# Sliding-window attention with top-1 experts on one core: q, k and v laid out by the host, bias added with the maximum

## The chip, the cores and the metric

The kernel runs on one core of one Trainium2 chip. The metric is device time in microseconds (us): the median of three timed runs of the kernel before is 689.68 us (685.45 to 692.1). The engines are TensorE (PE, with its weight loads PEld), VectorE (DVE), ScalarE (ACT), GpSimd (POOL) and SyncE (SP), which only issues transfers here.

## The reference

Eight batches, eight heads, 576 positions, 64 values a head. Scores get a bias that falls with distance, and only the 128 positions up to the query's own are seen. The rows of the result (4608 tokens x 512) go through a top-1 mixture of eight experts.

```python
scores = scale * np.matmul(q, k.transpose(0, 1, 3, 2))
rel = pos[:, None] - pos[None, :]
bias = slopes[:, None, None] * (-np.abs(rel).astype(np.float32))[None, :, :]
mask = (rel >= 0) & (rel < window)              # window = 128
scores = np.where(mask, scores + bias[None], -1000000000.0)
scores = scores - np.max(scores, axis=-1, keepdims=True)
attn = np.exp(scores)
attn = attn / (np.sum(attn, axis=-1, keepdims=True) + 1e-09)
x = np.matmul(attn, v)                          # then (tokens, heads * 64)
# per token: expert = argmax of cosine with expert_emb, gate = softmax at it
out[mask] = gate_w[mask, None] * (np.maximum(x[mask] @ w1[e], 0.0) @ w2[e])
```

## The kernel before, in words

The program has two stages. The first is attention with routing, 36 tiles of 128 query rows: per batch four tiles of 128 rows (the first of a batch is of kind "first", the others "full"), and per pair of batches one tile of kind "pair", which holds the last 64 rows of both. A tile is done in two halves of four heads, so there are 72 half tiles, called u below. The second stage runs the experts one after the other on the rows that routing scattered into a table in device memory. Part of the first expert's work (384 rows, "head") is done within the first stage, once 24 tiles are routed.

A half tile goes through these steps, each of which is a job of a planner:

- load (SP): q, k and v of the tile, 128 rows x 8 heads x 64, in runs of 64 values (`load`, L413 and L416).
- turn and copy (PE, then ACT or DVE): q and k are transposed four heads' pairs at a time by `prep_pe` (L492) into a PSUM bank and copied to SBUF by `prep_copy` (ACT L528, DVE L526), q with the scale.
- score (PE, `score_pe`): for two banks j a product writes the bias first (L592: the tables of `factors` for full and pair tiles, `tab_first` through the identity for first tiles), then L598 adds q times k, in fp32, over up to 256 key columns.
- merge (DVE, `merge_dve`, L607 and L610): the 256 columns hold the previous and the own tile's keys; a predicated copy folds them into 128, one per bank j.
- max (DVE, `max_dve`, L615): one reduction per bank, for two heads.
- exp (ACT, L622, one per head), flip (PE, L630, four transposes), phi (ACT, L481: the probabilities' high halves in fp16), plo (DVE, L484: the low halves), mask (POOL, L650 and L663: splits the folded block again), av (PE, `values_pe`, L698: 24 products), and the normalisation (DVE, L714 and L720).
- per tile: high and low halves of the result (ACT L734 or DVE L736, POOL L747), its square norm (ACT L743), a transposing transfer (SP, L751), the logits (PE, L757 and L761; DVE, L770), then for a group of tiles the routing (DVE and ACT, L825 to L854) and one scattering transfer per tile (POOL, L863).

The order on each engine is written by the planner (`Plan.run`): a list scheduler with a table of costs per job. At each step it looks at the engine whose next job can start first, and takes, among the jobs that can start within that engine's `SLACK` of the earliest, the one with the smallest due time. Due times are `STEP * u + 1000 * DUE[stage]`. Rings of buffers bound how far a job may run ahead; the PSUM rings of the first stage are `sc` (4 banks, two per half tile), `ps` (2 banks, shared by flip and av) and `pt` (2 banks, for turns, logits and small products). What the planner writes is a fixed order per engine; at run time each engine takes its instructions strictly in that order.

The costs and the order that touch the change most:

```python
J(f"score{u}", "PE", 750 if first else 1150 if pair else 1250, ...)
for j in range(2):
    J(f"merge{n}", "DVE", 0 if first else 202 if pair else 335, ...)
    J(f"max{n}", "DVE", 335, ..., after=[f"merge{n}"] + ([f"max{u}_0"] if j else []))
J(f"plo{u}", "DVE", 627, lambda a=a: probs_dve(*a), after=[f"phi{u}"], ...)
```

The second stage is not touched.

Of the kernel before, what the change touches and what calls it, by code (L numbers as in the profile page):

```python
# [13 lines left out]
F16 = mybir.dt.float16  # L14
BF16 = mybir.dt.bfloat16
F32 = mybir.dt.float32
# [13 lines left out]
SP_ = 2.0**15  # L30
# [22 lines left out]
STEP = 3038  # L53
SLACK = {'PE': 100, 'ACT': 100, 'DVE': 50, 'POOL': 400, 'SP': 300}
# [5 lines left out]
DUE = {'load': -8.2, 'loadv': 0.0, 'k': -6.5, 'q': -5.1, 'v': 2.1, 'score': -1.3, 'merge': 2.4, 'max': 1.7, 'exp': 3.0, 'flip': 3.2, 'phi': -1.8, 'plo': 7.8, 'mask': 6.2, 'av': -1.9, 'norm': 9.6, 'xhi': 2.6, 'xlo': 12.3, 'xnorm': 10.3, 'xdma': 16.1, 'logit': -1.8, 'route': 15.9, 'put': 19.8, 'place': 15.6, 'gap': 4.3}  # L60
# [8 lines left out]
SHARE = {'v': 0, 'x': 0.25, 'q': 0, 'k': 0, 'v2': 0, 'x2': 0.5, 'q2': 0.5, 'k2': 0.25}  # L69
# [88 lines left out]
def kernel(  # L158
# [12 lines left out]
    B, H, S, D = q.shape  # L171
    NTOK, DM = out.shape
    E, _, F = moe_w1.shape
# [7 lines left out]
    QS = -float(D) ** -0.5  # L181
# [34 lines left out]
    idb = const.tile([P, P], BF16, name="idb")  # L216
    nc.vector.tensor_copy(idb, ident)
# [54 lines left out]
    def merge_mask(kind):  # L272
        mk[kind] = const.tile([P, P], I32, name=f"mask_{kind}")
        nc.vector.tensor_scalar(mk[kind], rels[kind], 0.0, None, op0=ALU.is_ge)

    def first_table():
        tab = const.tile([P, H, P], BF16, name="tab_first")
        for h in range(H):
            nc.vector.tensor_scalar(tab[:, h, :], rels["full"], slopes[h], None, op0=ALU.mult)
        nc.gpsimd.affine_select(  # L280
            tab, tab, pattern=[[0, H], [-1, P]], compare_op=ALU.is_ge, fill=-NEG, base=0, channel_multiplier=1
        )
        tabs["first"] = tab

    def factors():
        at = const.tile([P, 2 * P], F32, name="at")
        nc.gpsimd.iota(at, pattern=[[1, 2 * P]], base=-P, channel_multiplier=0, allow_small_or_imprecise_dtypes=True)
        for kind in ("full", "pair"):
            tabs["row", kind] = const.tile([P, P], BF16, name=f"row_{kind}")
        tabs["col"] = const.tile([P, H // 2, 2 * P], BF16, name="col")  # L290
        for j in range(2):
            two, one = slice(64 * j, 64 * j + 2), slice(64 * j, 64 * j + 1)
            for kind in ("full", "pair"):
                row = tabs["row", kind]
                nc.vector.memset(row[two], 1.0)
                if kind == "full":
                    nc.vector.tensor_copy(row[one], at[one, P : 2 * P])
                else:
                    for i in range(2):
                        nc.vector.tensor_copy(row[one, i * REM : (i + 1) * REM], at[one, P : P + REM])  # L300
            for c in range(H // 2):
                x = slopes[2 * c + j]
                nc.vector.tensor_scalar(tabs["col"][two, c, :], at[two], -x, None, op0=ALU.mult)
                nc.gpsimd.memset(tabs["col"][one, c, :], x)
# [86 lines left out]
    def attention(actx):  # L391
# [11 lines left out]
        loaded = {}  # L403

        def load(T, which="qkv"):
            kind, b, t = tiles[T]
            r = loaded.setdefault(T, {})
            for nm, src in (("k", k), ("q", q), ("v", v)):
                if nm not in which:
                    continue  # L410
                x = ld.tile([P, H, D], F32, tag=f"ld{nm}", name=f"ld{nm}_{T}")
                if kind != "pair":
                    nc.sync.dma_start(x, src[b, :, t * P : (t + 1) * P, :].rearrange("h p d -> p h d"))  # L413
                else:
                    for i in range(2):
                        nc.sync.dma_start(  # L416
                            x[i * REM : (i + 1) * REM], src[b + i, :, NF * P : S, :].rearrange("h p d -> p h d")
                        )
                r[nm] = x

        load(0, "kq")
        load(1, "kq")
# [10 lines left out]
        bias_rel("full")  # L433
        first_table()
        merge_mask("full")
# [42 lines left out]
        qT, kT, vS = {}, {}, {}  # L478
# [6 lines left out]

        prep = {}

        def prep_pe(T, nm):
            x = loaded[T][nm].rearrange("p h d -> p (h d)")
            pt = bank("pt", [P, HP, P], name=f"pt{nm}_{T}")  # L490
            for hp in range(HP):
                nc.tensor.matmul(  # L492
                    pt[:, hp, :],
                    x[:, hp * P : (hp + 1) * P],
                    ident,
                    start=(hp == 0),
                    stop=(hp == HP - 1),
                    is_transpose=True,
                    skip_group_check=True,
                )  # L500
            prep[T, nm] = pt

        def k_blocks(T):
            kind, b, t = tiles[T]
            return [(b, 1), (b + 1, 1)] if kind == "pair" else [(b, t // 2)]

        def fill(T, nm):

            kind, b, t = tiles[T]
            if nm == "q":  # L510
                return [(qT.setdefault(T, {}), slice(0, P), slice(0, P), "q", P)]
            if kind == "pair":
                return [
                    (kT[x], slice(2 * P, 2 * P + REM), slice(i * REM, (i + 1) * REM), "k1", None) for i, x in enumerate(k_blocks(T))
                ]
            x = k_blocks(T)[0]
            return [(kT.setdefault(x, {}), slice(t % 2 * P, t % 2 * P + P), slice(0, P), f"k{x[1]}", 2 * P + REM * x[1])]

        def prep_copy(T, nm):
            scale = QS if nm == "q" else 1.0  # L520
            for at, dst, src, tg, w in fill(T, nm):
                if "x" not in at:
                    at["x"] = qk.tile([P, HP, w], F32, tag=tg, name=f"{nm}_{T}", bufs=KBUFS[tg])
                o_, i_ = at["x"][:, :, dst], prep[T, nm][:, :, src]
                if on_dve(T, nm):
                    nc.vector.tensor_scalar(o_, i_, scale, None, op0=ALU.mult)  # L526
                else:
                    nc.scalar.activation(o_, i_, AF.Copy, scale=scale)  # L528
            del prep[T, nm]

        def on_dve(T, nm):
            return share(T, SHARE[nm if T < LATE else nm + "2"])
# [10 lines left out]
        def v_hi(T):  # L543
            dst = vS[T][0][:, :, 0:D]
            if not share(T, SHARE["v" if T < LATE else "v2"]):
                nc.scalar.activation(dst, loaded[T]["v"], AF.Copy)
            else:
                nc.vector.tensor_copy(dst, loaded[T]["v"])

        def v_lo(T):  # L550
            tg = v_tag(T)
            lo = vp.tile([P, H, D], F16, tag=tg + "o", name=f"vo_{T}", bufs=VBUFS[tg])
            vS[T][1] = lo
            nc.gpsimd.tensor_tensor(lo, loaded[T]["v"], vS[T][0][:, :, 0:D], op=ALU.subtract)
# [13 lines left out]
        def score_pe(T, hf):  # L568
            kind, b, t = tiles[T]
            qx = qT[T]["x"]  # L570
            own = kT[k_blocks(T)[0]]
            if kind == "first":
                spans = [(slice(0, P), slice(0, P), own, slice(0, P))]
            elif kind == "pair":
                spans = [
                    (slice(i * REM, (i + 1) * REM), slice(0, P + REM), kT[x], slice(P, 2 * P + REM)) for i, x in enumerate(k_blocks(T))
                ]
            elif t % 2:
                spans = [(slice(0, P), slice(0, 2 * P), own, slice(0, 2 * P))]
            else:  # L580
                spans = [
                    (slice(0, P), slice(0, P), kT[b, t // 2 - 1], slice(P, 2 * P)),
                    (slice(0, P), slice(P, 2 * P), own, slice(0, P)),
                ]
            for j in range(2):
                ps = sc[T, hf, j] = bank("sc", [P, 2, 2 * P], name=f"sc{j}_{T}_{hf}")
                if kind == "first":
                    a_, b_ = idb, tabs["first"].rearrange("p (c j) k -> p j c k", j=2)[:, j, 2 * hf : 2 * hf + 2, :]
                else:
                    r = slice(64 * j, 64 * j + 2)  # L590
                    a_, b_ = tabs["row", kind][r], tabs["col"][r, 2 * hf : 2 * hf + 2, 0 : spans[-1][1].stop]
# [1080 lines left out]
```

## Time and profile before

| what | us |
|---|---|
| median of the three timed runs | 689.68 |
| the profiled execution's own time | 690.15 |
| its span, from the first to the last instruction | 688.4 |
| around the span | 1.75 |
| mean granted clock of TensorE, share of 2.4 GHz | 0.971 |
| busy over the span: PE, DVE, ACT, POOL | 643.3, 377.8, 340.8, 261.4 |

A row of busy time by stretch gives, for each engine, the time in which at least one of its instructions was under way, and their number in brackets; then the granted clock, the share of the transfer engines that was busy, and GB/s. A vector instruction's recorded duration reaches past the start of the next one where nothing makes that one wait, so a sum of durations is more than the time they take in a row; the starts of neighbours show the latter. PE products are recorded to their modelled end, some tenths of a us behind the next one's start.

### The profile page before, as it was taken

What the parts mean: (1) busy time and instruction counts of PE and PEld (TensorE: products, weight loads), DVE (VectorE), ACT (ScalarE), POOL (GpSimd) and SP (SyncE); (2) the same over time, 40 slices, a digit from 0 to 9 for tenths busy, and PEclk for the clock granted to TensorE, in tenths of its full rate; (3) what the DMA queues carried; (4) which work ended last, traced back from release to release, by engine and by line L of the source; (5) the groups of instructions that cost most, each with busy time, mean ns of one, the idle gap of its engine ahead of it and who ended that gap; (6) DMA issues with size and microseconds to landing.
All of it is one profiled execution on the core that took longest, in us unless ns stands there. A gap on an engine that the chain in (4) does not pass through costs nothing. (4 is left out here: it accounts for less than half of the span.)

```text
span 688.4 us, 15704 instructions
## 1 busy us (share of the span) xinstructions
PE 643.3 (93%) x6043; PEld 425.1 (62%) x6043; DVE 377.8 (55%) x974; ACT 340.8 (49%) x794; POOL 261.4 (38%) x472
## 2 busy tenths in 40 slices
PE   7999999999999988992999999999999999999993
PEld 4777767777776755641665467476584764754442
DVE  5877786776789969642335724344244255310250
ACT  5999888977887955410235523343243244210210
POOL 7667687767777837552010210120111112001011
PEclk9999999998999999886999999999999999999998
DMA  8588969886988895136999973934919545001000
GB/s 200 125 184 191 194 170 206 159 214 129 201 156 229 196 206 161 41 109 149 249 250 358 250 262 55 269 123 67 318 63 240 202 99 200 16 16 47 13 31 31
DMA packets 217676, 109.83 MB, mean 160 GB/s; under 512 B 195829, under 2 KB 195829, under 8 KB 217600
## 3 DMA queue, kind: packets, MB, share of 16 engines
q1 hardware_dynamic: 211760, 89.89, 55.7%
q0 software_dynamic: 5840, 18.92, 7.2%
q8 instruction: 48, 0.79, 0.5%
q14 instruction: 28, 0.23, 0.1%
HBM read 61.92 MB, written 28.12 MB: 131 GB/s over the span
## 5 line engine op out<-in xcount | busy, mean ns | idle before, releaser
L1374 PE MATMUL ps<-xT,w1h 128*128 128x272 f16 (+7 forms) x896 | 175.4, 296 | 13.4 <-DMA xT<-xs 12.2
L1374 PE MATMUL ps<-xT,w1l 128*128 128x272 f16 (+7 forms) x448 | 132.4, 296 | 0.0
L1374 PEld LDWEIGHTS <-w1h 128*128 128x128 f16 x896 | 88.2, 99 | 44.8 <-issue 14.1
L384 POOL DMA_INDIRECT out_dram<-y,ids x32 | 35.6, 1112 | 203.5 <-DVE y L1432 105.3
L1382 DVE SCALAR_TENSOR_TENSOR hl<-ps,hh 128x272 f16<-128x272 f32 (+7 forms) x112 | 51.7, 475 | 105.9 <-ACT hh L1384 99.5
L1384 ACT ACTIVATE hh<-ps 128x272 f16<-128x272 f32 (+7 forms) x112 | 45.6, 425 | 114.7 <-PE ps L1374 114.7
L622 ACT ACTIVATE pe<-sc,nm 128x128 f32<-128x128 f32 x288 | 87.7, 390 | 24.6 <-DVE nm L615 13.7
L1418 PE MATMUL ps<-w2h,hh 128*128 128x512 f16 (+1 forms) x264 | 98.4, 373 | 0.0
L1418 PE MATMUL ps<-w2l,hh 128*128 128x512 f16 (+1 forms) x264 | 98.4, 373 | 0.0
L1418 PE MATMUL ps<-w2h,hl 128*128 128x512 f16 (+1 forms) x264 | 98.4, 373 | 0.0
L1418 PEld LDWEIGHTS <-hh 128*128 128x128 f16 x528 | 51.5, 98 | 58.6 <-issue 0.8
L598 PE MATMUL sc<-k,q 64*128 64x128 f32 (+2 forms) x768 | 74.8, 339 | 0.5 <-ACT q L528 0.5
L484 DVE SCALAR_TENSOR_TENSOR pq<-ptp,pq 128x512 f16<-128x512 f32 x72 | 53.1, 738 | 20.3 <-ACT pq L481 18.1
L598 PEld LDWEIGHTS sc<-k,q 64*128 64x128 f32 (+1 forms) x768 | 51.0, 180 | 19.3 <-issue 16.4
L481 ACT ACTIVATE pq<-ptp 128x512 f16<-128x512 f32 x72 | 55.0, 764 | 14.4 <-PE ptp L630 8.8
L615 DVE TENSOR_REDUCE nm<-sc 128x2 f32<-128x256 f32 x144 | 58.5, 416 | 3.2 <-PE sc L598 2.9
L630 PE MATMUL ptp<-ident,pe 128*128 128x128 f32 x288 | 48.0, 287 | 8.0 <-ACT pe L622 3.6
L1349 DVE SCALAR_TENSOR_TENSOR w2l<-ws,w2h 128x1024 f16<-128x1024 f32 x28 | 33.9, 1223 | 36.2 <-ACT w2h L1351 36.0
L1374 PEld LDWEIGHTS <-w1l 128*128 128x128 f16 x448 | 44.1, 99 | 15.1 <-DVE w1l L1349 0.3
L1349 DVE SCALAR_TENSOR_TENSOR w1l<-ws,w1h 128x1024 f16<-128x1024 f32 x28 | 33.4, 1222 | 34.0 <-ACT w1h L1351 33.9
L747 POOL TENSOR_TENSOR gx<-xf,gx 128x512 f16<-128x512 f32 x36 | 42.7, 1187 | 19.7 <-ACT gx L734 8.5
L698 PE MATMUL av<-vh,mp 128*128 128x65 f16 (+1 forms) x512 | 49.0, 200 | 0.5 <-POOL mp L650 0.5
(233 smaller groups left out, 1174.1 us busy)
## 6 DMA issues: line engine op xcount, KB each, us to landing
ws<-moe_w_dram SPq DMA_DIRECT2D x56, 512.0 KB
ldk<-k_dram SPq DMA_DIRECT2D x32, 256.0 KB
ldq<-q_dram SPq DMA_DIRECT2D x32, 256.0 KB
ldv<-v_dram SPq DMA_DIRECT2D x32, 256.0 KB
stg<-moe_w_dram SPq DMA_DIRECT2D x16, 256.0 KB
xs<-zrow SPq DMA_DIRECT2D x3, 1092.2 KB
xs<-zrow SPq DMA_DIRECT2D x1, 1413.5 KB
xs<-zrow SPq DMA_DIRECT2D x1, 1285.0 KB
```

The costliest lines, as they stand in the source:

```text
L481: nc.scalar.activation(hi, ps, AF.Copy, scale=scale)
L484: nc.vector.scalar_tensor_tensor(lo, ps, scale, hi, op0=ALU.mult, op1=ALU.subtract)
L598: nc.tensor.matmul(sc[T, hf, j][o, l, w], qx[rows, hp, o], at["x"][rows, hp, kc], start=False, stop=(l == 1), skip_group_check=True)
L615: nc.vector.tensor_reduce(nm_t[T, hf][:, j, :], sc[T, hf, j][:, :, 0:P], axis=AX.X, op=ALU.min)
L622: nc.scalar.activation(pr_t[T, hf][:, 2 * l + j, :], ps[:, l, 0:P], AF.Exp, bias=nm[:, l : l + 1], scale=-1.0)
L630: nc.tensor.transpose(pt[:, i, :], pe[:, i, :], ident)
L698: nc.tensor.matmul(o_, a_, b_, start=False, stop=(n == last), skip_group_check=True)
L1349: nc.vector.scalar_tensor_tensor(lo_, x, SW, hi, op0=ALU.mult, op1=ALU.subtract)
L1374: nc.tensor.matmul(ps[:, :w], a[:, kt, fs], xx[:, b + kt, c0 : c0 + w], start=(n == 0), stop=(n == len(jobs) - 1))
L1382: nc.vector.scalar_tensor_tensor(hl[:, ft, c0 : c0 + w], ps[:, :w], 0.0, hi, op0=ALU.max, op1=ALU.subtract)
L1384: nc.scalar.activation(hi, ps[:, :w], AF.Relu)
L1418: nc.tensor.matmul(ps, x[:, ft, a * P : (a + 1) * P], w[:, ft, c], start=(n == 0), stop=(n == len(jobs) - 1))
```

## The change

- The host lays out q, k and v with numpy: q and k transposed, each tile's data in one run per partition. The turns and copies of q and k go (PE, ACT, DVE); q and k are loaded straight to where the products read them, q into 4 buffers of a tile, k into 3 of a batch.
- The bias products go. Two tables in bf16 (`bias_table`) hold the bias of each head after folding, and `max_dve` adds it with the maximum: one `tensor_tensor_reduce` per head writes (score + bias) * (-scale) back to PSUM and the minimum to `nm`. In the built program each is two instructions: the operation and a read of its accumulator (both appear as ISA).
- Both banks of a half tile are one tile of `sc` now (two tiles in place of four), and the four heads are folded by one predicated copy.
- The low halves of the probabilities are made, for each second half tile from u = 52 on (ten in all), by a product that subtracts the high halves in PSUM (`rest_pe`) and a copy on ACT, in place of the DVE operation.
- In pair tiles `av` uses full 128-column weights: POOL writes two masked tiles with a zeroed half each.
- PSUM rings: `sc` 2 x 2 banks, `ps` 3, `pt` 1. `STEP`, `SLACK`, `DUE` and `SHARE` have new values (a line or two shown); all high halves of the result before tile 26 are on ACT.

```diff
-SP_ = 2.0**15
+SP_ = 2.0**14
-RING = {'sc':'sc','pt':'pt','ptp':'ps','av':'ps','lg':'pt','misc':'pt'}
-BANKS = {'sc':4,'ps':2,'pt':2}
+RING = {'sc':'sc','ptp':'ps','av':'ps','lg':'pt','misc':'pt'}
+BANKS = {'sc':2,'ps':3,'pt':1}
-KBUFS = {"k0": 2, "k1": 2, "q": 3}
+KBUFS = {"k": 3, "q": 4}
-STEP = 3038
-SLACK = {'PE': 100, 'ACT': 100, 'DVE': 50, 'POOL': 400, 'SP': 300}
+STEP = 2454
+SLACK = {'PE': 43, 'ACT': 184, 'DVE': 46, 'POOL': 541, 'SP': 31}
-SHARE = {'v': 0, 'x': 0.25, 'q': 0, 'k': 0, 'v2': 0, 'x2': 0.5, 'q2': 0.5, 'k2': 0.25}
+SHARE = {'v': 0, 'x': 0, 'v2': 0, 'x2': 0.5, 'p': 0, 'p2': 0.5}
...
+    def bias_table(kind):
+        rel = rels[kind]
+        m = const.tile([P, P], I32, name=f"mask_{kind}")
+        wrap = const.tile([P, P], F32, tag="wrap", name=f"wrap_{kind}")
+        nc.vector.tensor_scalar(m, rel, 0.0, None, op0=ALU.is_ge)
+        nc.vector.tensor_scalar(wrap, rel, 0.0, float(WIN), op0=ALU.is_lt, op1=ALU.mult)
+        nc.vector.tensor_tensor(wrap, wrap, rel, op=ALU.add)
+        tab = const.tile([P, H, P], BF16, name=f"tab_{kind}")
+        for h in range(H):
+            nc.vector.tensor_scalar(tab[:, h, :], wrap, -slopes[h] / QS, None, op0=ALU.mult)
+        mk[kind], tabs[kind] = m, tab
...
-            for j in range(2):
-                ps = sc[T, hf, j] = bank("sc", [P, 2, 2 * P], name=f"sc{j}_{T}_{hf}")
...
-                nc.tensor.matmul(ps[:, :, 0 : b_.shape[-1]], a_, b_, start=True, stop=False, skip_group_check=True)
+            sc[T, hf] = bank("sc", [P, 2, 2, 2 * P], name=f"sc_{T}_{hf}")
...
-        def merge_dve(T, hf, j):
+        def merge_dve(T, hf):
             kind, b, t = tiles[T]
+            ps = sc[T, hf].rearrange("p j l c -> p (j l) c")
+            w = {"full": P, "pair": REM}.get(kind)
+            if w:
+                m = mk[kind][:, 0:w].unsqueeze(1).to_broadcast([P, 4, w])
+                nc.vector.copy_predicated(ps[:, :, 0:w], m, ps[:, :, P : P + w])
-            nc.vector.tensor_reduce(nm_t[T, hf][:, j, :], sc[T, hf, j][:, :, 0:P], axis=AX.X, op=ALU.min)
+            o_ = sc[T, hf][:, j, l, 0:P]
+            nc.vector.tensor_tensor_reduce(
+                o_, o_, tabs[tiles[T][0]][:, 4 * hf + 2 * l + j, :], -QS, BIG, ALU.add, ALU.min, nm_t[T, hf][:, j, l : l + 1]
+            )
...
+        def rest_pe(T, hf):
+            pq, pt = pq_t[T, hf]
+            nc.tensor.matmul(pt, minus, pq[:, :, :, 1], start=False, stop=True, skip_group_check=True)
+        def probs_lo(T, hf):
+            pq, pt = pq_t[T, hf]
+            if rest_on_pe(2 * T + hf):
+                hi_part(pq[:, :, :, 0], pt, SP_)
+            else:
+                lo_part(pq[:, :, :, 0], pq[:, :, :, 1], pt, SP_)
...
+                J(
+                    f"merge{u}", "DVE", 0 if first else 335 if pair else 600, lambda a=a: merge_dve(*a),
+                    after=[f"score{u}"], uses=[key], due=due("merge", u),
+                )
+                    for l in range(2):
+                        J(
+                            f"max{n}_{l}", "DVE", 245, lambda c=c, l=l: max_dve(*c, l),
+                            after=[f"max{n}_0" if l else f"merge{u}"] + ([] if l or not j else [(f"max{u}_0_0", ORDER)]),
...
+    qt = paired(np.asarray(q).transpose(0, 2, 1, 3)).reshape(-1, P, H // 2, 2 * D).transpose(0, 3, 2, 1)
+    kt = np.asarray(k).reshape(B, H // 2, 2, S // REM, REM, D).transpose(0, 2, 5, 3, 1, 4)
+    vt = paired(np.asarray(v).transpose(0, 2, 1, 3))
```

Three places in the built order. First DVE, first half of tile 10 before and of tile 16 after (both full): `sc0`, `sc1` and `sc` are scores, `nm` the minima, `tab_full` the bias table. Before:

```order
L484 SCALAR_TENSOR_TENSOR pq_9_0_1766<-ptp_9_0_1748,pq_9_0_1766 128x512 [waits Activation_49]
L607 COPY_PREDICATED sc0_10_0_1758<-mask_full_152,sc0_10_0_1758 128x2x128 [waits PE_49]
L770 COPY gl_0_719<-ptl_7_1779 128x16 [waits PE_49]
L615 TENSOR_REDUCE nm_10_0_1799<-sc0_10_0_1758 128x2 [waits DVE_49]
L825 TENSOR_SCALAR rc_0_1817<-gn_0_488 128x8
L607 COPY_PREDICATED sc1_10_0_1760<-mask_full_152,sc1_10_0_1760 128x2x128
L714 RECIPROCAL rs_9_0_1830<-av_9_0_1801 128x4 [waits PE_49]
L615 TENSOR_REDUCE nm_10_0_1799<-sc1_10_0_1760 128x2 [waits DVE_49]
```

After, on the same engine:

```order
L470 SCALAR_TENSOR_TENSOR pq_15_0_2345<-ptp_15_0_2326,pq_15_0_2345 128x512 [waits Activation_49]
L714 COPY gl_1_1817<-ptl_12_2357 128x16 [waits PE_49]
L537 COPY_PREDICATED sc_16_0_2339<-mask_full_139,sc_16_0_2339 128x4x128
L658 RECIPROCAL rs_14_1_2408<-av_14_1_2369 128x4 [waits PE_49]
L543 ISA sc_16_0_2339,nm_16_0_2410<-sc_16_0_2339,tab_full_144 128x128 [waits DVE_49]
L543 ISA nm_16_0_2410 128x1
```

Two folds and two reductions have become one fold and four pairs of operation and accumulator read; three more pairs like the last one follow straight behind, and the operation of each of those waits, in the built program, for the accumulator read just ahead of it.

Second, PE in the middle of the stage (`ptk` and `ptp` are the banks of a turn of k and of a flip, `sc0`, `sc1` scores). Before:

```order
L492 MATMUL ptk_18_2850<-ident_68,ldk_18_2339 128x128 x4
L630 MATMUL ptp_16_0_2861<-ident_68,pe_16_0_2844 128x128 x4
L592 LDWEIGHTS row_pair_172
L592 MATMUL sc0_17_0_2874<-col_173,row_pair_172 128x2x192
L592 LDWEIGHTS row_pair_172
L592 MATMUL sc1_17_0_2876<-col_173,row_pair_172 128x2x192
L598 MATMUL sc0_17_0_2874<-k_11_1815,q_17_2763 64x192
```

After, on PE, from a flip on:

```order
L560 MATMUL ptp_0_3131<-ident,pe_0_3101 128x128 x4
L522 MATMUL sc_0_3141<-k_1755,q_2604 128x256 x4
L560 MATMUL ptp_1_3169<-ident,pe_1_3159 128x128 x4
L627 LDWEIGHTS erow
L627 MATMUL av_1_3176<-eone,erow 128x4
```

Turns and bias products are gone; a flip is followed by scores, and these by the next flip or av.

Third, PE at the end of the attention stage, from the last av product on (`ps_head` is the head expert's output bank, `w1`, `w2` its weights). Before:

```order
L698 LDWEIGHTS mp_1_6354
L698 MATMUL av_1_6409<-vh_4877,mp_1_6354 64x65
L969 LDWEIGHTS hh_head
L969 MATMUL ps_head_6459<-w2h_4951,hh_head 128x512
L969 LDWEIGHTS hh_head
L969 MATMUL ps_head_6459<-w2l_4952,hh_head 128x512
```

After:

```order
L642 LDWEIGHTS mp_35_1_5630
L642 MATMUL av_1_5664<-vh_4947,mp_35_1_5630 128x65
L891 LDWEIGHTS w1h_4388
L891 MATMUL ps_head_5645<-x_head,w1h_4388 128x384
L891 LDWEIGHTS w1l_4389
L891 MATMUL ps_head_5645<-x_head,w1l_4389 128x384
```

Before, all 96 products of the head's first layer stood ahead of the last av; after, 44 of them stand behind it, ahead of the 72 of the second layer.

## Rows read from the trace of the kernel before

**Rows 1.** Busy time by stretch of the span: us, busy time and instructions of PE, PEld, DVE, ACT and POOL, granted clock, transfer share, GB/s.

```profile
20.00:120.00 100.00, 96.73 (x1380) 75.39 (x1380) 78.97 (x237) 88.51 (x237) 71.64 (x116) 1.00 0.82 178
120.00:240.00 120.00, 113.83 (x1613) 87.32 (x1609) 97.87 (x299) 99.47 (x267) 91.14 (x156) 0.97 0.84 184
20.00:240.00 220.00, 210.56 (x2991) 162.71 (x2989) 176.84 (x535) 187.98 (x503) 162.78 (x270) 0.98 0.83 181
240.00:292.00 52.00, 45.09 (x517) 30.54 (x517) 38.84 (x112) 28.07 (x73) 27.17 (x44) 0.91 0.60 136
292.00:326.00 34.00, 21.76 (x114) 10.22 (x113) 11.95 (x62) 2.39 (x8) 12.87 (x31) 0.75 0.48 128
340.00:650.00 310.00, 308.81 (x2066) 187.84 (x2065) 120.83 (x176) 103.85 (x170) 41.00 (x62) 1.00 0.55 161
```

**Rows 2.** The longest wait of PE from 20 to 240 us: who waited for whom, us in total, times, longest.

```profile
PE ptp L630 <- ACT pe L622: 2.1, 3, 0.8
```

**Rows 3.** PE in order of time near 132 us: start, us recorded, line, out<-in.

```profile
131.75 0.63 PE L630 MATMUL ptp<-ident,pe 128*128 128x128 f32 x4
132.22 0.60 PE L492 MATMUL ptq<-ident,ldq 128*128 128x128 f32 x4
132.65 0.38 PE L592 MATMUL sc<-tab_first,idb 128*128 128x256 bf16 x2
132.97 0.71 PE L598 MATMUL sc<-k,q 64*128 64x128 f32 x8
```

**Rows 4.** Busy time of single PE lines from 20 to 240 us: first the bias products (L592), then the turns (L492, four to a turn).

```profile
20.00:240.00 220.00, 24.12 (x124) 0.98 0.83 181
20.00:240.00 220.00, 37.94 (x252) 0.98 0.83 181
```

**Rows 5.** Busy time of single DVE lines from 20 to 240 us, in this order: folds of full tiles (L607), folds of pair tiles (L610), maxima (L615), copies of q and k (L526), high halves (L736), low halves of the probabilities (L484).

```profile
20.00:240.00 220.00, 32.62 (x83) 0.98 0.83 181
20.00:240.00 220.00, 2.96 (x12) 0.98 0.83 181
20.00:240.00 220.00, 49.65 (x124) 0.98 0.83 181
20.00:240.00 220.00, 4.13 (x6) 0.98 0.83 181
20.00:240.00 220.00, 5.76 (x8) 0.98 0.83 181
20.00:240.00 220.00, 45.85 (x62) 0.98 0.83 181
```

**Rows 6.** Groups of DVE instructions over the span: shapes, count, busy us, mean ns of one, idle before.

```profile
L607 DVE COPY_PREDICATED sc<-mask_full,sc 128x256 f32<-128x256 int32 x96 | 37.8, 421 | 2.7 <-PE sc L598 1.9 <-PE ptp L630 0.8
L610 DVE COPY_PREDICATED sc<-mask_pair,sc 128x128 f32<-128x128 int32 x16 | 3.9, 293 | 1.6 <-PE sc L598 1.6
```

**Rows 7.** DVE in order of time: two neighbours near 128 us; the smallest write without a source, near 1 us; two small instructions of the routing, each of which waits for the one ahead, near 304 us.

```profile
128.14 0.50 DVE L610 COPY_PREDICATED sc<-mask_pair,sc 128x128 f32<-128x128 int32 x2
128.54 0.76 DVE L615 TENSOR_REDUCE nm<-sc 128x2 f32<-128x256 f32 x2
...
0.85 0.06 DVE L226 MEMSET eone<- 3x4 bf16 x1 [0.85 <-PEq L1661]
...
303.53 0.16 DVE L829 TENSOR_TENSOR rz<-rz,gn 128x2 f32<-128x2 f32 x1
303.73 0.16 DVE L830 TENSOR_TENSOR rz<-rz,ry 128x2 f32<-128x2 f32 x1
```

**Rows 8.** Busy time by stretch, columns as in rows 1.

```profile
220.00:240.00 20.00, 18.94 (x267) 14.59 (x267) 19.46 (x50) 19.11 (x50) 18.12 (x27) 1.00 0.89 208
240.00:260.00 20.00, 16.90 (x183) 12.00 (x183) 14.40 (x45) 12.82 (x34) 6.12 (x8) 0.91 1.02 198
260.00:280.00 20.00, 17.15 (x196) 10.92 (x195) 16.74 (x47) 10.54 (x30) 15.06 (x29) 0.91 0.44 133
```

**Rows 9.** ACT and POOL: the busy time of ACT's copies of q and k (L528) from 20 to 240 us; two neighbours on ACT near 123 us; the group of POOL's masks of pair tiles.

```profile
20.00:240.00 220.00, 34.12 (x59) 0.98 0.83 181
...
122.79 0.63 ACT L528 ACTIVATE k<-ptk 128x512 f32<-128x512 f32 x1
123.27 0.78 ACT L481 ACTIVATE pq<-ptp 128x512 f16<-128x512 f32 x1
...
L663 POOL TENSOR_SCALAR_AFFINE_SELECT tails<-pq 64x256 f32<-64x256 f32 x16 | 7.0, 436 | 5.6 <-DVE pq L484 4.2 <-DVE rs L714 0.6 <-DVE rz L828 0.3
```

**Rows 10.** The start: DVE makes the first table, POOL masks it (a group of one), PE turns the first k, DVE takes the first maximum.

```profile
2.66 1.18 DVE L279 TENSOR_SCALAR tab_first<-rel_full 128x128 bf16<-128x128 f32 x8 [0.87 <-POOL rel_full L268]
...
L280 POOL TENSOR_SCALAR_AFFINE_SELECT tab_first<-tab_first 128x1024 bf16<-128x1024 bf16 x1 | 1.1, 1098 | 1.3 <-DVE tab_first L279 1.3
...
6.19 0.60 PE L492 MATMUL ptk<-ident,ldk 128*128 128x128 f32 x4
...
10.32 0.75 DVE L615 TENSOR_REDUCE nm<-sc 128x2 f32<-128x256 f32 x2
```

**Rows 11.** The end of the attention stage: the last av products on PE, the last group's first scattering transfer on POOL, and the wait of the second stage's first product.

```profile
291.50 0.25 PE L698 MATMUL av<-vh,mp 128*64 128x65 f16 x2
...
311.58 0.98 POOL L863 DMA_INDIRECT xs<-gx,di  x1 [1.61 <-issue]
...
PE ps L1374 <- DMA xT<-xs: 12.2, 1, 12.2
```

More of the change, by code (lines that the diff above doesn't have):

```diff
@@ L170 @@
     nc = tc.nc
-    B, H, S, D = q.shape
     NTOK, DM = out.shape
+    B, D = k.shape[0], P // 2
+    H, S = DM // D, NTOK // B
     E, _, F = moe_w1.shape
@@ L276, in first_table @@
     def first_table():
         tab = const.tile([P, H, P], BF16, name="tab_first")
-        for h in range(H):
-            nc.vector.tensor_scalar(tab[:, h, :], rels["full"], slopes[h], None, op0=ALU.mult)
         nc.gpsimd.affine_select(
-            tab, tab, pattern=[[0, H], [-1, P]], compare_op=ALU.is_ge, fill=-NEG, base=0, channel_multiplier=1
+            tab, tabs["full"], pattern=[[0, H], [-1, P]], compare_op=ALU.is_ge, fill=NEG, base=0, channel_multiplier=1
         )
         tabs["first"] = tab
[L285 to L290, printed above, removed]
-        for j in range(2):
[L292 to L304, printed above, removed]
@@ L401, in attention, with load @@
         hp_ = actx.enter_context(tc.tile_pool(name="head", bufs=1))
-        loaded = {}
-        def load(T, which="qkv"):
+        loaded, qT, kT = {}, {}, {}
+        def load(T, nm):
             kind, b, t = tiles[T]
[L407 to L422, printed above, removed]
+            if nm == "q":
+                qT[T] = qk.tile([P, HP, P], F32, tag="q", name=f"q_{T}", bufs=KBUFS["q"])
+                nc.sync.dma_start(qT[T], q[T].rearrange("p (a c) -> p a c", a=HP))
+            elif nm == "k":
+                for x in (b, b + 1) if kind == "pair" else (b,):
+                    if x not in kT:
+                        kT[x] = qk.tile([P, S // REM, HP, REM], F32, tag="k", name=f"k_{x}", bufs=KBUFS["k"])
+                    c = slice(P // REM * t, S // REM if kind == "pair" else P // REM * (t + 1))
+                    nc.sync.dma_start(kT[x][:, c], k[x].rearrange("p (n a c) -> p n a c", a=HP, c=REM)[:, c])
+            else:
+                loaded[T] = x = ld.tile([P, H, D], F32, tag="ldv", name=f"ldv_{T}")
+                nc.sync.dma_start(x, v[T].rearrange("p (h d) -> p h d", h=H))
+        for T in range(2):
+            for nm in "kq":
+                load(T, nm)
         emb = const.tile([E, DM], F32, name="emb")
@@ L433, in attention @@
         bias_rel("full")
+        bias_table("full")
         first_table()
-        merge_mask("full")
         warm(WARM)
@@ L484, in lo_part @@
             nc.vector.scalar_tensor_tensor(lo, ps, scale, hi, op0=ALU.mult, op1=ALU.subtract)
[L486 to L532, printed above, removed]
         def v_tag(T):
@@ L1061, in attention @@
                 first = kind == "first"
-                dep = [f"copy_q{T}"] + [f"copy_k{x}" for x in k_tiles(T)] + (["tab_pair"] if pair else []) + ([] if first else ["factors"])
-                keys = [("sc", u, j) for j in range(2)]
+                dep = [f"load_q{T}"] + [f"load_k{x}" for x in k_tiles(T)] + (["tab_pair"] if pair else [])
+                key = ("sc", u)
                 J(
-                    f"score{u}", "PE", 750 if first else 1150 if pair else 1250, lambda a=a: score_pe(*a), makes=[(RING["sc"], x) for x in keys],
+                    f"score{u}", "PE", 530 if first else 900 if pair else 1080, lambda a=a: score_pe(*a), makes=[(RING["sc"], key)],
@@ L1084, in attention @@
+                for j in range(2):
+                    c, n = a + (j,), f"{u}_{j}"
+                    J(
+                        f"exp{n}", "ACT", 502, lambda c=c: exp_act(*c), after=[f"max{n}_0", (f"max{n}_1", -251)] + ([(f"exp{u}_0", ORDER)] if j else []),
                         makes=[] if j else [("pe", ("pe", u))], uses=[key, ("nm", u), ("pe", u)],
```

196 lines of the change are left out of this document (90 added, 106 removed).

## The prediction

> **What bounds the kernel now.** I read busy time by stretch first. From 340 us on PE is busy 308.8 of 310 us: the second stage is bound by PE, and the change leaves its instructions as they are, so I carry it over whole. Everything at stake lies before 292 us. From 20 to 240 us PE is busy 210.6 of 220 us (96%), ACT 188.0 (85%), DVE 176.8 (80%), POOL 162.8 (74%) [rows 1]. Then the waits of PE: the longest in these 220 us adds up to 2.1 us [rows 2]. So PE is the bound of the attention stage, by its own work. The low halves of the probabilities, one DVE operation per half tile, count 62 there [rows 5]: the stage does 62 of 72 half tiles in 220 us, 3.55 us each. From 240 to 292 us the last eight half tiles stand between scattering transfers and the head's products, and from the last av product at 291.5 us on there is a chain of latencies, not a bound by work: routing, the last transfers at 311.6 us, then 12.2 us until the first rows of the second stage have landed [rows 11]. I take that end, some 34 us, as unchanged.
>
> The profiled execution took 690.15 us, 0.5 us over the median of 689.68; all sums are made against it.
>
> **PE: what goes.** A turn of q or k takes 0.43 us from its start to the next product's, the bias products 0.32 us [rows 3]. From 20 to 240 us there are 252 / 4 = 63 turns, 63 x 0.43 = 27.1 us (the recorded 37.9 holds the modelled ends), and bias products for 62 half tiles, 62 x 0.32 = 19.8 us [rows 4]. PE falls from 210.6 to about 164 us; six subtracting products of the low halves (those of u from 52 to 63) give back 1 to 3 us. That is 22% of the stage's bound. It becomes time only as far as the next engine allows.
>
> **DVE: what goes and what comes.** From 20 to 240 us the folds, maxima, copies of q and k and the high halves go: 32.62 + 2.96 + 49.65 + 4.13 + 5.76 = 95.1 us, and 6 of 62 low halves, 4.4 us [rows 5]. 176.8 - 95.1 - 4.4 = 77.3 us stay. In come:
>
> Folds of four heads. 128 columns are recorded with 293 ns, 256 with 421 [rows 6], so 512 with about 677; neighbours start 0.09 us before the recorded end (two of 293 ns start 0.20 us apart [rows 7]), which leaves 0.59 to 0.68 us. With 0.62: 83 / 2 x 0.62 = 25.7 us, and 6 in pair tiles at 0.33, 2.0 us. The fold is thus no saving to speak of: a fixed part less per half tile.
>
> Bias and maximum. 62 x 4 = 248 pairs of operation and accumulator read, which no row shows. The operation streams 128 columns from PSUM, as the fold of 128 does: 0.20 us to the next start [rows 7]. The read costs between 0.06 us (the smallest write without a source) and 0.16 us (a small operation with one) [rows 7]. The built order shows that three in four operations wait for the read just ahead, so its whole time counts, and a dependent neighbour starts another 0.04 us late (0.16 us recorded, 0.20 us apart [rows 7]). A pair therefore costs 0.30 to 0.40 us; I take 0.32, since the read has no source in memory. The first of four waits for the fold: 0 to 0.13 us, as something stands between or not; I take 0.05. 62 x (4 x 0.32 + 0.05) = 82.5 us, with bounds of 74 and 107.
>
> DVE then has 77.3 + 25.7 + 2.0 + 82.5 = 187.5 us for the same 62 half tiles (178 to 215). The work removed from PE lands on an engine that had 80%: DVE, not PE, is the bound after the change.
>
> **The other two.** ACT loses 59 copies of q and k at 0.48 us from start to start [rows 9], 28 us, and takes 8 high halves and 6 low halves at about 0.6, 8 us: 168 us. POOL gains two masks of 0.44 us [rows 9] and two zeroings and loses one mask in each of six pair half tiles, under 1 us each: some 166 us. Neither is the bound at 200 us. Transfers fall: runs of 64 values become whole rows per partition; no wait of PE on them is worth counting before [rows 2], so I give this nothing.
>
> **From work to time.** PE ran at 96% where it was the bound, and DVE itself reached 19.46 of 20 us from 220 to 240 us [rows 8]. But its order is strict: a half tile's fold waits for the scores, the low half for ACT, and the pairs' waits cannot be filled. I take 93%: 187.5 / 0.93 = 202 us in place of 220, 18 us gained. The start: before, the first maximum came at 10.3 us after turns and copies; k is there at 6.2 us, the scores take 0.7 us, and the first table, with three more operations in front, is masked by about 6 us [rows 3, 10]; 3 us gained (0 to 4). 240 to 292 us: 8 x 0.32 + 3 x 0.43 = 3.9 us of PE go, but transfers and the head's work set much of it; 2 us (0 to 6). Moving 44 head products behind the last av costs 44 x about 0.17 = 7.5 us of PE there, beside a chain of latencies in which PE is busy only 21.8 of 34 us [rows 1]: hidden, with 5 us to spare; if the chain were that much shorter it would show. Sum: 18 + 3 + 2 = 23, so 690.15 - 23 = 667 us.
>
> **Where a rule of the skill speaks against it.** The pair's price is the weak point. In the trace two independent operations of 293 ns start 0.20 us apart [rows 7]. The Trainium skill ("VectorE: DVE Perf Modes", section "The DRAIN you can't avoid") has the next operation start only when the pipeline is empty, and advises to minimise the number of operations; the trace does not agree for independent neighbours, and no run so far shows an accumulator read. What it would make of the sum is the first rival.
>
> **Rivals.**
>
> 1. Drained pairs (slower). If the read starts only when the operation has ended, a pair costs 0.29 + 0.04 + 0.06 to 0.16 + 0.04 = 0.43 to 0.53 us. At 0.44, DVE has 105 + 62 x (1.76 + 0.05) = 217 us, 234 at 93%: 14 us lost, 5 won at start and end, 699 us; at 0.53 some 720. It decides from 0.41 us per pair on, where 248 pairs eat all that PE gives back. For it: the waits in the built order, eight instructions in place of two. Against it: neighbours overlap wherever they are independent. Chance 0.10.
>
> 2. The pace is set by the chain, not by DVE. At 202 us four engines stand at 81 to 93%, and each half tile passes PE, DVE, ACT, PE, ACT, DVE, POOL and PE in strict orders, with two score buffers. For it: ACT and DVE stood at 85% and 80% beside a PE at 96% [rows 1], so nothing shows four engines all near full. Against it: `ps` has a third bank, and before, four engines summed to 738 us of work in 220 us, now to 686. At 3.4 us per half tile 62 take 211 us: 9 + 5 gained, 676 us. Chance 0.20.
>
> 3. PE's clock. With PE at 165 of 202 us there is more idle time in it. The granted clock was 0.91 where PE was busy 17 of 20 us, and 0.75 where it was busy 22 of 34 [rows 1, 8], that is, a part of the time at 1.2 in place of 2.4 GHz. At 0.91 PE needs 181 us, still under DVE; it decides below 165 / 202 = 0.82; at 0.75 the stage takes 220 us again and only start and end gain: 685 us. Against it: a slow PE becomes busy, and from 20 to 120 us 97% went with 1.00. The Trainium skill ("TensorE: Matmul & The Clock Gate", section "What's actually happening") says that the throttled state is the default and activity releases it; these rows agree. Chance 0.06.
>
> 4. Cheap pairs and a dense DVE: 178 us at 96% is 185, and start and end give 7 more: 35 + 7 = 42, some 648 us. Chance 0.14.
>
> The forecast as worked out, 656 to 678 us: 0.50.
>
> **How the numbers follow.** The range takes in the fourth case's edge and ends just above no change: 648 to 692; the first rival is left out, and a little of the fourth. About 1% (7 us) is what a measurement tells from no change here. Faster: 0.50 + 0.14 + 0.16 of case 2 + 0.02 of case 3 = 0.82. Same: 0.09, from cases 2 and 3 and the near edge of case 1. Slower: 0.09, case 1 for the most part.
>
> **What would show it.** Right: between 20 and 220 us DVE is the busiest engine, at over 90%, PE near 80%; a pair's starts lie 0.30 to 0.36 us apart; the fold is recorded with about 0.68 us; the last av comes near 268 us, and from there to the second stage's first product it is again some 34 us; the second stage keeps its 362 us. Wrong: pairs at 0.41 us or more (rival 1); DVE under 88% with waits on PE or ACT spread over it (rival 2); a granted clock under 0.85 in that stretch (rival 3); a stretch from the last av to the second stage that has grown, or a second stage that has changed its length, which no case here has.

## The result: 0.9% slower, and the profile after

| | before | after |
|---|---|---|
| median, us (20 runs each) | 688.51 | 693.66 |
| ratio, 95% interval | | 1.0085 (1.0057 to 1.0113) |
| profiled span, us | 688.4 | 693.6 |
| mean granted clock | 0.971 | 0.938 |
| last av product, first product of the second stage, us | 291.5, 322.6 | 294.1, 326.2 |

The forecast was 667 us. The 23 us that it saw won before 292 us are not there: the attention stage ends 2.6 us later than before, the stretch behind it is 1 us longer (32.1 for 31.1), the second stage 1.5 us (367.4 for 365.9).

Busy time by stretch of the kernel after, columns as in [rows 1]:

```profile
20.00:240.00 220.00, 179.73 (x2426) 134.10 (x2426) 189.98 (x820) 164.32 (x434) 155.40 (x270) 0.89 0.65 173
240.00:292.00 52.00, 40.92 (x484) 28.62 (x484) 39.45 (x158) 37.08 (x93) 37.10 (x68) 0.85 0.70 156
340.00:650.00 310.00, 307.73 (x2063) 187.61 (x2061) 123.75 (x183) 105.11 (x173) 38.83 (x62) 1.00 0.58 165
```

DVE is now the busiest engine from 20 to 240 us, but with 86%, and no engine is near full. PE is busy 31 us less at a granted clock of 0.89 in place of 0.98. In these 220 us 60 half tiles pass (480 instructions of the pairs' line, eight to a half tile): 3.67 us each, against 3.55.

Two half tiles on DVE in order of time, with what ended an idle time in brackets (L543: the operation and the read of its accumulator, L537 fold, L470 low half, L658 and L664 normalisation):

```profile
60.31 0.30 DVE L543 CUSTOM_DVE_ANT_0 sc<-sc,tab_full 128x128 f32<-128x128 f32 x1
60.52 0.14 DVE L543 DVE_READ_ACCUMULATOR2_ANT nm<- 128x1 f32 x1
60.70 0.30 DVE L543 CUSTOM_DVE_ANT_0 sc<-sc,tab_full 128x128 f32<-128x128 f32 x1
60.91 0.14 DVE L543 DVE_READ_ACCUMULATOR2_ANT nm<- 128x1 f32 x1
60.91 0.42 DVE L664 TENSOR_TENSOR xf<-av,rs 128x256 f32<-128x256 f32 x1
61.25 0.72 DVE L470 SCALAR_TENSOR_TENSOR pq<-ptp,pq 128x512 f16<-128x512 f32 x1
61.87 0.69 DVE L537 COPY_PREDICATED sc<-mask_full,sc 128x512 f32<-128x512 int32 x1
62.48 0.17 DVE L658 RECIPROCAL rs<-av 128x4 f32<-128x4 f32 x1
62.60 0.30 DVE L543 CUSTOM_DVE_ANT_0 sc<-sc,tab_full 128x128 f32<-128x128 f32 x1
62.81 0.14 DVE L543 DVE_READ_ACCUMULATOR2_ANT nm<- 128x1 f32 x1
62.81 0.17 DVE L714 COPY gl<-ptl 128x16 f32<-128x16 f32 x1
62.99 0.30 DVE L543 CUSTOM_DVE_ANT_0 sc<-sc,tab_full 128x128 f32<-128x128 f32 x1
63.21 0.14 DVE L543 DVE_READ_ACCUMULATOR2_ANT nm<- 128x1 f32 x1
64.10 0.30 DVE L543 CUSTOM_DVE_ANT_0 sc<-sc,tab_full 128x128 f32<-128x128 f32 x1 [0.75 <-ACT pe L552]
```

Two things are to be seen. From 60.31 to 60.70 us a pair takes 0.39 us: the read starts 0.21 us behind its operation, but the next operation only 0.18 us behind the read. Where other work of DVE stands behind the read, as at 60.91 and 62.81, that work starts with the read and fills the wait. Other work stands behind 105 of the 240 pairs from 20 to 240 us; of the other 135, 121 take 0.35 to 0.43 us. And the third operation of the second half tile, for which DVE is free at 63.35, starts at 64.10 when the exps of two other heads have ended. The waits from 20 to 240 us (who for whom, us in total, times, longest), first DVE's longest, then ACT's and PE's:

```profile
DVE sc L543 <- ACT pe L552: 15.7, 25, 0.8
```

```profile
ACT pe L552 <- DVE nm L543: 31.3, 47, 3.0
```

```profile
PE ptp L560 <- ACT pe L552: 17.5, 30, 1.3
```

DVE waits for exps, the exps wait for DVE's minima, and PE's flips wait for the exps. The fold, recorded with 0.69 us, is as forecast.

### The profile page after: what moved, and what is told of

Same layout as the page of the kernel before. It is cut to its first block, busy times and chain, and to the rows that moved or that the text cites. A ratio compares the mean times of both kernels' runs of the same rounds, so it can differ in the third digit from the quotient of the medians.

```text
span 693.6 us, 14909 instructions
## 1 busy us (share of the span) xinstructions
PE 614.3 (89%) x5493; PEld 398.1 (57%) x5493; DVE 396.1 (57%) x1318; ACT 325.7 (47%) x743; POOL 259.2 (37%) x488
## 5 line engine op out<-in xcount | busy, mean ns | idle before, releaser
L370 POOL DMA_INDIRECT out_dram<-y,ids x32 | 33.4, 1045 | 207.2 <-DVE y L1376 98.6
L560 PE MATMUL ptp<-ident,pe 128*128 128x128 f32 x288 | 59.9, 321 | 44.8 <-ACT pe L552 26.9
L522 PE MATMUL sc<-k,q 64*128 64x256 f32 (+2 forms) x640 | 84.7, 411 | 0.0
L560 PEld LDWEIGHTS ptp<-ident,pe 128*128 128x128 f32 x288 | 36.7, 156 | 60.2 <-ACT pe L552 45.8
L467 ACT ACTIVATE pq<-ptp 128x512 f16<-128x512 f32 x82 | 61.6, 753 | 19.0 <-PE ptp L560 13.3
L543 DVE CUSTOM_DVE_ANT_0 sc<-sc,tab_full 128x128 f32<-128x128 f32 x192 | 57.1, 298 | 21.6 <-ACT pe L552 17.8
L642 PE MATMUL av<-vh,mp 128*128 128x65 f16 x512 | 53.0, 201 | 1.9 <-POOL mp L592 1.5
L1295 ACT ACTIVATE w1h<-ws 128x1024 f16<-128x1024 f32 x28 | 28.4, 1052 | 44.8 <-DMA ws<-moe_w_dram 44.7
```

What stands on the lines that cost most here:

```text
L370: ins = nc.gpsimd.indirect_dma_start(out[:, :], bass.IndirectOffsetOnAxis(ap=ids, axis=0), y, None, bounds_check=NTOK - 1, oob_is_err=False)
L467: nc.scalar.activation(hi, ps, AF.Copy, scale=scale)
L522: nc.tensor.matmul(sc[T, hf][o, j, l, w].rearrange("p (n c) -> p n c", c=REM), qT[T][rows, hp, o], kT[x][rows, kc, hp, :], start=True, sto ...
L543: nc.vector.tensor_tensor_reduce(o_, o_, tabs[tiles[T][0]][:, 4 * hf + 2 * l + j, :], -QS, BIG, ALU.add, ALU.min, nm_t[T, hf][:, j, l : l + 1]
L560: nc.tensor.matmul(pt[:, i, :], pe[:, i, :], ident, start=(i == 0), stop=(i == 3), is_transpose=True, skip_group_check=True)
L642: nc.tensor.matmul(o_, a_, b_, start=False, stop=(n == last), skip_group_check=True)
```

## The experiments

Each run is compared with runs of the kernel before on the same chip; chips differ (its median was 681.7, 690.4 and 681.9 us beside experiments 1 to 4, 5 to 7 and 8 to 10), so ratios are compared, not times. Theory A: in the program that was built, 239 of the 288 operations wait for DVE itself, most (152) for the accumulator read just ahead, and 41 for an exp. None of these waits is in the data, except those for the fold.

**1. Tiles of their own.**

```diff
-            o_ = sc[T, hf][:, j, l, 0:P]
-            nc.vector.tensor_tensor_reduce(o_, o_, ..., nm_t[T, hf][:, j, l : l + 1])
+            nm_t[T, hf, i] = sm.tile([P, 1], F32, tag=f"nm{i}", ...)
+            pr_t[T, hf, i] = pp.tile([P, P], F32, tag=f"pe{i}", ...)
+            nc.vector.tensor_tensor_reduce(pr_t[T, hf, i], sc[T, hf][:, j, l, 0:P], ..., nm_t[T, hf, i])
```

> Each head's operation writes to an SBUF tile of its own and its minimum to a tile of its own, and the exp works in place on that tile; the order of the jobs stays nearly as it was. In the program no operation waits for the accumulator read ahead or for an exp any more. Theory A (false waits: the operation is taken to touch the whole score tile and the whole tile of minima, so it waits for the read ahead and for exps of other heads, and DVE is what sets the pace): a pair falls from 0.39 to about 0.30 us from start to start, 0.09 x 240 = 22 us from 20 to 240 us, and the 15.7 us of DVE's waits for exps there go; up to 38 us less, of which the next engine (ACT, PE at a lower clock) takes some back: 660 to 675 us. Rival B (the pace is set by the chain through four engines, and DVE's waits only show it): the waits move elsewhere, 686 to 694 us. Rival C (the granted clock of PE, 0.89 in that stretch, sets the pace): time within 5 us of the changed kernel's unless the clock goes back to 0.97.

Measured: ratio 0.9553 (0.9504 to 0.9601), median 651.22 us. The last av product comes at 250.6 us, 43 us earlier than after the change (on a chip where the kernel before is 1% faster; 37 us earlier than in experiment 4, on the same chip); the clock from 20 to 240 us is 0.95. A holds, and its gain is larger than expected, since the read turns out to cost nothing (experiment 8 shows the rows).

**2. Bias on PE again, one maximum per half tile.**

```diff
+                nc.tensor.matmul(sc[T, hf][:, j, :, 0 : b_.shape[-1]], a_, b_, start=True, stop=False, ...)
-            nc.vector.tensor_tensor_reduce(...)            # four pairs
+            nc.vector.tensor_reduce(raw, sc[T, hf][:, :, :, 0:P], axis=AX.X, op=ALU.max)
+            nc.vector.tensor_scalar(nm_t[T, hf], raw, -QS, None, op0=ALU.mult)
```

> The changed kernel with its layout by the host, but the bias products on PE again and one maximum over the four heads of a half tile (512 columns) with one small scaling operation in place of four pairs. Theory A (DVE with its pairs is the bound): DVE loses 4 x 0.39 us and some 0.26 us of waits and gains about 0.72 + 0.20 per half tile, 0.9 us; PE gains 0.32 us; the pace falls from 3.67 us per half tile to that of PE or ACT at 2.9 to 3.1, the time to 650 to 672 us. Rival B (chain through four engines): the pace stays near 3.5 us, 680 to 692. Rival C (clock): PE has more work and fewer gaps, so the granted clock from 20 to 240 us goes from 0.89 to 0.95 or more, and the time falls with it.

Measured: ratio 0.9974 (0.9946 to 1.0003), median 681.0 us; only durations of single instructions are read from its profile, whose run took 690.71 us. What A expected did not come: the pairs are gone, and the time is that of before, within rival B's range. In order of time (first POOL, then DVE; L569 is the small scaling operation):

```profile
122.13 1.12 POOL L509 TENSOR_TENSOR vo<-ldv,vh 128x512 f16<-128x512 f32 x1
122.20 1.07 DVE L569 TENSOR_SCALAR nm<-mx 128x4 f32<-128x4 f32 x1
```

An operation of four columns takes 1.07 us and ends with POOL's; over the run this line takes 137 ns at least, 2.8 us at most. So this run did not yet test what it was made for.

**3. The old numbers of the planner.** Only `STEP`, `SLACK` and `DUE` are those of the kernel before.

> The changed kernel with the step, the slacks and the due times of the kernel before. Theory A (false waits on DVE set the pace): they stay, so the time stays within 1%: 687 to 700 us. Rival D (the new table of due times is what costs the gain, for example by setting the exps behind other work on ACT): 670 to 682 us.

Measured: ratio 1.027 (1.0213 to 1.0327). DVE's waits for exps from 20 to 240 us (in total, times, longest):

```profile
DVE sc L543 <- ACT pe L552: 22.1, 34, 1.3
```

The new numbers are worth 1.8% (1.027 / 1.0085); rival D falls. Theory A's 1% does not hold either: the waits did not stay, they grew with the old order.

**4. Minima of their own, scores in place.** Of the first experiment's edit, only the `nm_t` lines.

> Only the minima are in tiles of their own, one per head; the operation still writes the score tile in place. Theory A with the score tile as the link: the operations still wait for the ones ahead and for exps, pairs stay 0.39 us apart and DVE's waits for exps stay near 16 us from 20 to 240 us; 690 to 698 us. A' (the tile of minima is the link): pairs at 0.30 us, no waits for exps, 660 to 680 us.

Measured: one run, 688.23 us, 1.010 of the median before. Pairs 0.39 us apart, and the waits for exps are there:

```profile
DVE sc L542 <- ACT pe L551: 17.0, 27, 0.8
```

The tile of minima is not the link.

**5. As 2, the raw maxima in PSUM.**

```diff
+            raw = sc[T, hf][:, 0, 0, P : P + 4].rearrange("p (j l) -> p j l", j=2)
```

> As the second experiment (bias on PE, one maximum and one scaling operation per half tile), but the four raw maxima are written to spare columns of the score bank, so that the scaling operation reads PSUM. In the second experiment this operation, SBUF to SBUF, took 0.14 to 2.8 us, mean 0.49, and its long ones ended with a two-source operation of POOL. Theory A2 (that contention set DVE's pace there): the scaling operation falls to about 0.2 us each time, 0.3 us of 3.6 per half tile go, and the time falls to 655 to 668 us. Rival B (the chain through the engines sets the pace of any such version): 676 to 684 us.

Measured: ratio 0.9806 (0.9744 to 0.9869), median 675.25 us, somewhat less gain than expected. The scaling operation by shape from 20 to 240 us (count, busy us, mean ns, idle before), in experiment 2 and here:

```profile
L569 DVE TENSOR_SCALAR nm<-mx 128x4 f32<-128x4 f32 x61 | 30.0, 492 | 0.4
```

```profile
L569 DVE TENSOR_SCALAR nm<-sc 128x4 f32<-128x4 f32 x65 | 10.2, 157 | 0.4
```

With its source in PSUM it takes 0.16 us each time, and the kernel gains 1.7% on experiment 2. So the change with its bias left on PE, all its other parts together, is worth about 2%; in experiment 2 the long scaling operations hid it. Set against the 688.5 us of before, the interval is 671 to 680 us: it reaches into rival B's range and not into that of A2. What part the chain through the engines has here stays open.

**6. Products that keep PE busy.**

```diff
+            for _ in range(2):
+                nc.tensor.matmul(pt, ones, ones.unsqueeze(1).to_broadcast([P, 4, P]), start=True, stop=True, ...)
```

> The changed kernel with two products of 512 columns, whose result is overwritten, ahead of each flip, where PE mostly waits for the exp. They add 2 x 0.21 us of PE work per half tile. Rival C (the lower granted clock, 0.89 from 20 to 240 us against 0.98 before, costs the time): the clock goes to 0.95 or more and the time falls by 5 us or more against the changed kernel, ratio to the kernel before under 1.0. Theory A (DVE with its false waits sets the pace, the low clock follows from PE's idle time): the clock rises and the time stays, ratio 1.00 to 1.015.

Measured: ratio 1.0053 (1.003 to 1.0077), which overlaps that of the change. Busy time from 20 to 240 us:

```profile
20.00:240.00 220.00, 191.21 (x2584) 136.39 (x2584) 192.56 (x831) 166.87 (x442) 157.59 (x272) 0.96 0.69 176
```

With PE busy 191 us in place of 180 the clock is up from 0.89 to 0.96; DVE and the time stay. The low clock follows from PE's idle time, and what it costs (0.3%) is within the intervals, as far as the added products themselves cost nothing. Rival C falls.

**7. A fourth buffer and 215 ns for a pair in the planner.** `bufs=4`, `XBUFS = 12` on top of experiment 1.

> The first experiment (a tile of its own for each head's biased scores and minimum) with a fourth buffer for these tiles in place of one buffer of result rows, and with 215 in place of 245 ns for a pair in the planner's table. If waits for a free buffer still hold the operations of a half tile back, 3 to 8 us less than the first experiment (ratio 0.943 to 0.952); if the four engines at 84 to 91% of their time are the limit, the same within 0.5%.

Measured: ratio 0.9594 (0.9534 to 0.9653), no gain over 0.9553.

**8. Only the place of the output.**

```diff
-                o_, o_, tabs..., nm_t[T, hf][:, j, l : l + 1]
+                pr_t[T, hf][:, i, :], sc[T, hf][:, j, l, 0:P], tabs..., nm_t[T, hf][:, j, l : l + 1]
-                nc.scalar.activation(pr_t[T, hf][:, i, :], ps[:, l, 0:P], AF.Exp, ...)
+                nc.scalar.activation(pr_t[T, hf][:, i, :], pr_t[T, hf][:, i, :], AF.Exp, ...)
```

> Only the place of the operation's output is changed against the changed kernel: it goes to the SBUF tile that the exp wrote before (one tile per half tile, as there), and the exp works on it in place; the minima stay in their one tile. In the program no operation waits for an exp and 54 of 288 wait for DVE (239 and 41 in the changed kernel). Theory A in its narrow form (the in-place write to the score tile in PSUM is what ties the operations to each other and to the exps): as the first experiment, ratio 0.950 to 0.962, pairs 0.21 us apart. A' (the single tiles of the first experiment were needed as well): ratio over 0.98.

Measured: ratio 0.9578 (0.9554 to 0.9601), median 653.52 us, the same as experiment 1 within the intervals. Three pairs on DVE in order of time, then the busy time from 20 to 240 us:

```profile
64.79 0.28 DVE L544 CUSTOM_DVE_ANT_0 pe<-sc,tab_full 128x128 f32<-128x128 f32 x1
65.00 0.08 DVE L544 DVE_READ_ACCUMULATOR2_ANT nm<- 128x1 f32 x1
65.00 0.28 DVE L544 CUSTOM_DVE_ANT_0 pe<-sc,tab_full 128x128 f32<-128x128 f32 x1
65.21 0.08 DVE L544 DVE_READ_ACCUMULATOR2_ANT nm<- 128x1 f32 x1
65.21 0.29 DVE L544 CUSTOM_DVE_ANT_0 pe<-sc,tab_full 128x128 f32<-128x128 f32 x1
65.42 0.08 DVE L544 DVE_READ_ACCUMULATOR2_ANT nm<- 128x1 f32 x1
```

```profile
20.00:240.00 220.00, 197.03 (x2831) 147.71 (x2832) 202.28 (x949) 194.67 (x513) 186.02 (x324) 0.94 0.82 206
```

Without the wait the next operation starts with the read: a pair takes 0.21 us, not 0.39. DVE's waits for exps are gone; its longest wait from 20 to 240 us is now

```profile
DVE pq L470 <- ACT pq L467: 4.6, 12, 1.1
```

68 half tiles pass in place of 60 (272 exps, four each), 3.24 us each, and all four engines are busy 85 to 92%. The edit brings two more things, and the traces show neither as the gain: the exps read SBUF, but are recorded with 0.39 us each in place of 0.37; and the score tile comes free before the exps, but the trace of the changed kernel shows no wait of a score product for an exp. The order on the engines is nearly that of the changed kernel (the same for DVE's first 1000 of 1320 instructions and all of POOL's). So the cause is settled: the in-place write to the score tile in PSUM. Why the program ties operations on this tile together, and not on an SBUF tile of the same cut, was not tried, nor how the gain divides between the two kinds of wait.

**9. All low halves on DVE.** `'p2': 0` in `SHARE`.

> The changed kernel with all low halves of the probabilities on DVE: no subtracting products and no copies on ACT in their place. If DVE sets the pace, ten operations of 0.65 us more on it cost 3 to 7 us: ratio 1.01 to 1.02. If the chain through the engines sets the pace late in the stage, where the transfers and the head's work stand, no difference: ratio 1.00 to 1.01.

Measured: ratio 1.0288 (1.026 to 1.0316), more than ten operations can cost. Last av product and first product of the second stage, on PE:

```profile
292.29 0.23 PE L642 MATMUL av<-vh,mp 128*128 128x65 f16 x2
...
331.70 0.64 PE L1318 MATMUL ps<-xT,w1h 128*128 128x288 f16 x2 [6.31 <-DMA xT<-xs]
```

The stretch behind the last av is 39.4 us, against 32.1 after the change. So about half of the loss of 2% (14 us) against the changed kernel lies in the order of the end of the stage; what in it is late was not settled, nor where the other half lies, which the ten operations could explain.

**10. Both heads of a bank in a row.** On top of experiment 1, the operations in the order of the banks.

> The first experiment with the four operations in the order of the score banks (both heads of the first bank, then both of the second), so that the first exps can start after two pairs in place of three. If the way through the engines still costs something, 2 to 6 us less than the first experiment: ratio 0.945 to 0.952; if the engines at 84 to 91% are the limit, 0.952 to 0.962.

Measured: ratio 0.9687 (0.9654 to 0.972), slower than experiment 1, against both expectations. Its last av comes at 258.7 us, 8 us later, and the second stage starts 36 us behind it, in place of 32. Earlier exps brought nothing; what in the other order costs the time was not settled.

## Why the prediction was wrong, step by step

- **DVE in place of PE as the bound: right.** PE is busy 31 us less from 20 to 240 us (180 us, not the 164 forecast, at the lower clock), and the place of DVE's output alone decides the time (experiment 8).
- **The step that failed first is the 93%, in "187.5 / 0.93 = 202 us".** For 62 half tiles the kernel took 62 x 3.67 = 227 us, not 202, and this 25 us is nearly the whole error. To divide it, I count each DVE instruction of the trace from its start to its neighbour's, less the idle time between them. DVE then works 189.7 us for 60 half tiles and is idle 30.0 us; for 62 that is 196 and 31 us, where the forecast had 187.5 and 14. So 17 of the 25 us are idle time, 86% in place of 93%. The waits for exps, 15.7 us or 0.26 us per half tile, are in no term: I counted what the operations wait for on DVE, and not what they wait for on ACT, though both stand in the same built order. Of the rest of the idle time, 4.5 us are gaps of some 0.03 us ahead of an operation, most of them behind the read that it waits for.
- **The other step that failed is "176.8 - 95.1 - 4.4 = 77.3 us stay".** It makes DVE's work too small, 8.5 of the 25 us. The 95.1 us are recorded durations, which reach past the start of the next instruction, but what comes in was priced from start to start. A maximum of the kernel before, recorded with 0.39 us, makes room for the next instruction after 0.31:

```profile
67.03 0.39 DVE L615 TENSOR_REDUCE nm<-sc 128x2 f32<-128x256 f32 x1
67.34 0.41 DVE L720 TENSOR_TENSOR xf<-av,rs 128x256 f32<-128x256 f32 x1
```

Counted from start to start, the five rows of 95.1 us occupy 82.6 us and the six low halves 3.9, so 90 us stay, not 77.3. After the change everything but folds and pairs is 91.7 us, for 60 half tiles. The pairs came out under their term, which hides part of this.
- **The pair at 0.32 us came out, but by luck.** Operation, read and gap take 75.6 us for 240 pairs, 0.315 us each, so the term of 82.5 us measured 62 x 4 x 0.315 = 78 us. But no pair takes that. With the next operation right behind, it takes 0.39 us (0.21, then a read recorded with 0.14, then a gap of 0.03 to 0.04), near the upper bound of 0.40, since the read, without a source, is not as short as I took it. With other work behind, it takes 0.22 us: so it is for 59 of the 60 last pairs of a half tile, and in 46 more the wait that "cannot be filled" was filled. The wait is 0.18 of the 0.39 us; where nothing waits, the read costs no time of its own.
- **The small terms.** The start gained 2.4 us of my 3 (first operation at 7.97 us, first maximum before at 10.32 [rows 10]); the fold's 0.69 us is as forecast. The 2 us from 240 to 292 us went the way of the rest.
- **Rivals.** The result lies where rival 1 said, slower, but not from the point that it named: with its share of the waits for exps, 0.315 + 15.7 / 240, a pair comes to 0.38 us, under its 0.41. Its mechanism, a drained pipeline, is not there: within the changed kernel the same two instructions take 0.39 us with the wait and 0.22 without. The Trainium skill ("VectorE: DVE Perf Modes", section "The DRAIN you can't avoid") has the next operation wait until the pipeline is empty, but adds that one that is not held starts earlier, which the prediction left out and these rows bear out; it also reports a chain of copies that took the same time with a semaphore after each as with one after the last, and there these rows differ. Rival 3's clock did fall, to 0.89, not below its 0.82, and experiment 6 shows no cost of it beyond the intervals. Rival 2's sign came, DVE under 88% with waits for ACT, and the pace was slower than its 3.4 us; experiment 8 shows that these waits hang on the place of one output.
- **The end.** I took it at 34 us, unchanged; it was 31.1 and became 32.1. That it can move by 7 us with one number (experiment 9) was not in my sum.

## What to carry to other kernels

Read the waits of a built program one by one, and ask of each whether the data needs it: an in-place write to a tile that several steps share can tie them all. A wait for DVE's own read costs 0.18 us here where the next operation stands right behind it, and nothing where other work lies between, so look at the order before pricing it. Do not take recorded durations that overlap off a sum to which distances between starts are added. An engine busy 86% can be the bound, if what fills the rest is waits in a ring; experiment 8 turns a loss of 0.9% into a gain of 4.2% by moving one output, and beats both kernels.

## What was not expected of the hardware

- A read of DVE's accumulator is free where nothing waits for it: it starts 0.21 us behind its 128-column operation, and the next operation starts with it. Its record is 0.14 us in the changed kernel, whether the next one waits or not, and 0.08 us in experiment 8, where the operation writes to SBUF.
- A vector operation from SBUF to SBUF can last as long as POOL's work beside it: four columns took 1.07 us beside a two-source POOL operation of 1.12 us, and 0.16 us on the average with a PSUM source. In experiment 2 all 23 of these operations that took over 0.4 us end within 0.06 us of an operation on POOL, 12 of them two-source. The Trainium skill ("GPSIMD Engine Reference", section "1. Specifications") names contention on the SBUF interfaces shared with DVE, for DVE instructions in a 2-port mode or with two SBUF inputs; these rows agree in what happens; which mode this one-input operation runs in, no row shows.
